# Expert tiles routed in two rounds: six tiles from the first three batches during attention, the rest beside those tiles

## The chip, the cores and the metric

The kernel runs on one core of a Trainium2 chip. A core has five engines, each with an instruction queue of its own that is worked in order: TensorE (PE in the profile; its weight loads are PEld), VectorE (DVE), ScalarE (ACT), GpSimd (POOL) and SyncE (SP), which here only issues transfers. Engines wait for one another through semaphores; the DMA engines move data beside all of them. TensorE reads its operands from the on-chip memory (SBUF) and writes its sums to PSUM, eight banks of 2 KB a partition. The metric is the time of one execution in microseconds on the device. `L12` in a line of the profile is line 12 of the kernel's file; the letters ahead of it name the engine.

## The reference

Sparse attention (half of the heads attend to the last 32 positions, half to every 32nd), and behind it a mixture of eight experts. A token takes the expert that its own logits prefer, or, where its local gate says so, the expert of the token before it. It then passes through that one expert and is scaled by that expert's probability.

```python
batch, n_heads, seq, head_dim = (8, 8, 576, 64)        # attention; float32 throughout
mask_local = (rel >= 0) & (rel < 32)                   # heads 0 to 3
mask_strided = (rel >= 0) & (pos[None, :] % 32 == pos[:, None] % 32)   # heads 4 to 7
attn = softmax(where(mask, q @ k.T / 8, -1e9))
x = (attn @ v).transpose(0, 2, 1, 3).reshape(8, 576, 512)

logits = x @ w_gate                                    # 8 experts
local_gate = sigmoid(x @ w_local)
for b in range(B):
    prev_e = -1
    for s in range(S):
        fresh_e = argmax(logits[b, s])
        e = fresh_e if s == 0 or local_gate[b, s] < 0.5 else prev_e
        prev_e = e
        p = softmax(logits[b, s])
        out[b, s] = p[e] * (relu(x[b, s] @ w1[e]) @ w2[e])   # w1[e] 512x1024, w2[e] 1024x512
```

## The kernel before

**Attention** (`attention`, L145) goes through 8 batches of 8 units (both counted from 0 below). A unit is a pair of heads and half of the sequence's blocks. Per unit, TensorE computes the scores (`L241`), ScalarE takes the exponential (`L245`), VectorE multiplies by the mask (`L248`), TensorE multiplies with the values (`L287`), and VectorE normalises into rows `xl` or `xs` (`L295`, `L297`, `L298`). The loop is written in a staggered order: step n issues the scores of unit n, the values of unit n-2, and, for every second unit, the transposes `turn_x` (`L321`, `L329`; ScalarE copies them to `xT`, `L323`, `L332`) of unit n-3. Each group of two pairs is stored to the DRAM table `xd` of 4608 rows of 512 numbers (`L306`, `L310`); a batch has six loads and six stores, all issued by SyncE. Behind a batch's last transposes stand its gates (`L334` to `L372`): eight matmuls with the gate weights (`L340`), a copy `gl` (`L343`), six small matmuls that turn the logits to token rows (`L346`), and VectorE's softmax and argmax. They leave `probs` (eight probabilities a token) and `codes`, a number from which the running maximum later tells each token's expert. Transposes, values and gates share one PSUM pool (`psT`, two tiles of two banks); scores have `psS`, also two tiles of two banks.

**Routing** (`route`, L397) runs once, after the last batch. It turns the codes to rows (`L442`, copied by `L446`), finds each token's expert by a running maximum (`L448`) and marks it one-hot (`L454`, `hot`), counts with a running sum (`cum`), rounds each expert's count up to whole tiles of 128 tokens, and gives each token a slot in the list of tiles. Then it inverts that list by 48 matmuls into a table (`L515`): `lane` marks a token's place within its tile, `put` its tile (`at`, `L505`) times its number and times its probability (`pt`, `L507`). The results are `gi` (which row of `xd` each slot gathers), `si` (which row of the output it writes, out of range for an empty slot), `ps_slot` (its probability) and `et` (the expert of each tile and the number of tiles used). After it a check (`bounds`) decides whether all sums were in a safe range; if not, everything would be done again more carefully, which does not happen here.

**Experts** (`experts`, L526) go tile by tile: two weight transfers of 2 MB (`L543`, `L545`, SyncE, from four buffers each), a gather of 128 rows (`L547`, GpSimd), four transposes (`L554`) and a copy (`L556`, VectorE), the hidden layer (`L566`, 64 matmuls counting the two passes that an fp32 one is recorded as; ScalarE's Relu `L568`), the output layer (`L574`), the scaling (`L577`) and a scatter to the output (`L578`, GpSimd). The loads of tile j+2 are issued ahead of tile j. At most 43 tiles can be needed and 36 always are; from tile 36 on each stands behind a branch on the count `used`:

```python
    for j in range(NT):
        if j == NT_MIN:
            used = nc.values_load(et[0:1, NT:NT + 1], min_val=NT_MIN, max_val=NT,
...
        if j + 2 < NT:
            load(j + 2)
        ...
            with tc.If(used > j):
                hidden(j)
                output(j)
```

The pools of routing and of the experts follow one another in the same part of SBUF and PSUM (the inner `ExitStack`s of `passes`, L105), so the first weight transfer waits until routing and the check are done with theirs. The order of each engine's queue is settled before the run by a scheduler from the program's order and its dependences.

## Time and profile before

| | us |
|---|---|
| median of three runs (866.14 to 867.58) | 867.15 |
| the profiled execution | 866.83 |
| its span | 865.10 |
| TensorE busy | 792.3 |
| VectorE busy | 170.2 |
| ScalarE busy | 154.1 |
| GpSimd busy | 90.1 |

The span is the time from the first to the last instruction that the profile shows; the execution's time lies 1.73 above it. Busy times are those of single engines and overlap. The rows that matter for the change, stage by stage and instruction by instruction, stand in the prediction. Four of its views need a word. The page's slices cut the span into 40 equal parts of 21.6 us, each a digit in tenths. A row of the windows gives `from:to`, the length, and each engine's busy time with its count, then TensorE's granted clock as a share of full speed, the share of 16 DMA engines busy, and GB/s. A row of the chain or of the timeline gives start and length of an instruction or of a run of like instructions, and in brackets the idle time before it and what ended it. A row of the groups ends with busy time, mean ns of one, and idle time before with its releaser.

### The profile page before, as it was taken

How to read it: one execution, taken by the hardware profiler on the slowest of the kernel's cores; microseconds unless marked ns; L12 is line 12 of the kernel's file. 1: busy time of each engine (PE TensorE's matmuls, PEld its weight loads, DVE VectorE, ACT ScalarE, POOL GpSimd, SP SyncE). 2: the span in 40 equal slices, each digit the busy share in tenths (PEclk: the TensorE clock that was granted, in tenths of full speed). 3: DMA queues.
4: the chain of work that ended last, by engine and by line, in shares of the span. 5: the costliest groups of instructions: out<-in, count | busy, mean ns of one | idle time of the engine just before them, and what ended most of it. 6: DMA issues, size and time to landing. Idle time of an engine off the chain costs nothing.

```text
span 865.1 us, 12699 instructions
## 1 busy us (share of the span) xinstructions
PE 792.3 (92%) x5324; PEld 605.3 (70%) x5324; DVE 170.2 (20%) x470; ACT 154.1 (18%) x250; POOL 90.1 (10%) x105
## 2 busy tenths in 40 slices
PE   6999999973859999999999999999999999997990
PEld 6777788762847777777777777777777777765860
DVE  4565665558320000000000000000000000000000
ACT  3444444430001111111111111111111111110110
POOL 1000000001030001111111111111111111110000
PEclk9999999985559999999999999999999999998995
DMA  9667776110079999999898989898989899886860
GB/s 363 237 236 236 236 236 233 58 56 1 0 276 399 399 400 399 400 399 375 320 339 312 340 313 336 318 339 315 331 311 341 307 338 322 330 318 216 299 227 8
DMA packets 91172, 242.63 MB, mean 280 GB/s; under 512 B 4638, under 2 KB 13854, under 8 KB 91104
## 3 DMA queue, kind: packets, MB, share of 16 engines
q1 hardware_dynamic: 83936, 220.92, 70.9%
q0 software_dynamic: 6640, 20.72, 6.3%
q8 instruction: 46, 0.75, 0.3%
q14 instruction: 22, 0.18, 0.1%
q10 hardware_dynamic: 528, 0.07, 0.0%
HBM read 222.81 MB, written 19.92 MB: 281 GB/s over the span
## 4 chain that ended last, share of the span: by engine, by line
issue 41%; PE 31%; DMA 15%; POOL 4%; ACT 3%; DVE 3%; POOLq 0%; SPq 0%; ACTq 0%
DMA out_dram<-y,si 13%; PE tps L287 9%; PE hps L566 5%; PE yps L574 5%; PE sps L241 4%; POOL out_dram L578 2%; PE tab L515 2%; POOL xg L547 2%; PE tps L340 2%; PE tps L329 1%; ACT xT L332 1%; ACT xT L323 1%; DMA xg<-xd,gi 1%; PE tps L346 1%; PE tps L321 1%
## 5 line engine op out<-in xcount | busy, mean ns | idle before, releaser
L566 PEld LDWEIGHTS hps<-xgT,w1t 128*128 128x128 f32 x2560 | 294.8, 193 | 17.8 <-issue 17.7
L566 PE MATMUL hps<-xgT,w1t 128*128 128x128 f32 x2560 | 295.0, 276 | 0.0
L574 PE MATMUL yps<-w2t,hT 128*128 128x512 f32 x640 | 281.3, 592 | 0.0
L574 PEld LDWEIGHTS yps<-w2t,hT 128*128 128x128 f32 x640 | 118.5, 190 | 133.9 <-issue 133.9
L556 DVE COPY xgT<-xps 128x512 f32<-128x512 f32 x43 | 29.6, 691 | 564.0 <-PE xps L554 503.0
L568 ACT ACTIVATE hT<-hps 128x512 f32<-128x512 f32 x80 | 47.8, 597 | 263.5 <-PE hps L566 263.5
L577 ACT ACTIVATE y<-yps,ps_slot 128x512 f32<-128x512 f32 x40 | 27.5, 687 | 264.9 <-PE yps L574 258.6
L578 POOL DMA_INDIRECT out_dram<-y,si x40 | 40.0, 1000 | 319.8 <-ACT y L577 305.5
L241 PE MATMUL sps<-qt,kt 64*128 64x96 f32 (+2 forms) x704 | 63.5, 295 | 6.6 <-DMA kt<-in_k_dram 6.6
L547 POOL DMA_INDIRECT xg<-xd,gi x43 | 42.3, 983 | 226.2 <-PE xps L554 200.9
L241 PEld LDWEIGHTS sps<-qt,kt 64*128 64x128 f32 (+2 forms) x704 | 47.8, 189 | 19.7 <-issue 11.2
L245 ACT ACTIVATE e<-sps 128x576 f32<-128x576 f32 (+1 forms) x64 | 41.8, 653 | 46.3 <-PE sps L241 35.5
L287 PE MATMUL tps<-vlt,e 128*96 128x96 f32 x384 | 40.9, 257 | 0.8
L554 PE MATMUL xps<-ident,xg 128*128 128x128 f32 x172 | 28.5, 295 | 13.8 <-DMA xg<-xd,gi 13.5
L287 PE MATMUL tps<-vst,e 108*108 108x108 f32 (+1 forms) x320 | 40.1, 273 | 0.7
L287 PEld LDWEIGHTS tps<-vlt,e 128*96 128x96 f32 x384 | 35.8, 167 | 4.0 <-ACT xT L323 2.3
L287 PEld LDWEIGHTS tps<-vst,e 108*108 108x108 f32 (+1 forms) x320 | 34.6, 180 | 4.4 <-ACT xT L323 2.2
L554 PEld LDWEIGHTS xps<-ident,xg 128*128 128x128 f32 x172 | 21.7, 152 | 16.9 <-issue 15.9
L248 DVE TENSOR_TENSOR e<-e,maskL 128x576 f32<-128x576 f32 x32 | 24.3, 758 | 36.3 <-ACT e L245 36.3
L515 PE MATMUL tab<-put,lane 96*128 96x86 f32 x96 | 20.8, 422 | 11.1 <-DVE put L507 11.1
L515 PEld LDWEIGHTS tab<-put,lane 96*128 96x128 f32 x96 | 20.6, 333 | 11.2 <-issue 11.2
L248 DVE TENSOR_TENSOR e<-e,maskS 108x648 f32<-108x648 f32 (+1 forms) x32 | 24.2, 757 | 16.8 <-ACT e L245 16.8
(133 smaller groups left out, 250.5 us busy)
## 6 DMA issues: line engine op xcount, KB each, us to landing
w1t<-in_w_dram SPq DMA_DIRECT2D x43, 2048.0 KB
w2t<-in_w_dram SPq DMA_DIRECT2D x43, 2048.0 KB
kt<-in_k_dram SPq DMA_DIRECT2D x16, 608.0 KB
qt<-in_q_dram SPq DMA_DIRECT2D x16, 576.0 KB
vlt<-in_vl_dram SPq DMA_DIRECT2D x8, 780.0 KB
vst<-in_vs_dram SPq DMA_DIRECT2D x8, 650.0 KB
xd<-xl SPq DMA_DIRECT2D x8, 576.0 KB
xd<-xs SPq DMA_DIRECT2D x24, 108.0 KB
```

What stands on the lines that cost most here:

```text
L241: nc.tensor.matmul(ps[0:kb, h, i * w:(i + 1) * w], lhsT=kt[r, u.i2, c:c + kb], rhs=qt[r, u.i2, c:c + w], start=True, stop=True)
L245: nc.scalar.activation(ev, ps[0:kb, :, 0:m * w], Act.Exp, bias=0.0, scale=1.0 / DH ** 0.5)
L248: nc.vector.tensor_tensor(blocks(ev, m), blocks(ev, m), mask, op=Alu.mult)
L287: nc.tensor.matmul(ps[0:w, h, o:o + w], lhsT=u.e[0:kb, h, i * w:(i + 1) * w], rhs=vt[0:kb, u.i2, u.t0 + i, c:c + w], start=True, stop=True)
L515: nc.tensor.matmul(tab, lhsT=lane[:, i], rhs=put[:, i], start=(i == 0), stop=(i == CM - 1))
L547: nc.gpsimd.indirect_dma_start(out=t["x"], out_offset=None, in_=xd, in_offset=bass.IndirectOffsetOnAxis(ap=gi[:, j:j + 1], axis=0))
L554: nc.tensor.transpose(ps[:, kk * P:(kk + 1) * P], t["x"][:, kk * P:(kk + 1) * P], ident)
L556: nc.vector.tensor_copy(t["xT"], ps)
L566: nc.tensor.matmul(ps[:, i], lhsT=t["w1"][:, kk, c], rhs=t["xT"][:, kk * P:(kk + 1) * P], start=(kk == 0), stop=(kk == DK - 1))
L568: nc.scalar.activation(t["hT"][:, g * HB:(g + 1) * HB], ps, Act.Relu)
L574: nc.tensor.matmul(ps, lhsT=t["hT"][:, kk], rhs=t["w2"][:, kk, :], start=(kk == 0), stop=(kk == FK - 1))
L578: nc.gpsimd.indirect_dma_start(out=out, out_offset=bass.IndirectOffsetOnAxis(ap=si[:, j:j + 1], axis=0), in_=y, in_offset=None, bounds_che ...
```

## The change

Routing is done twice by one generator, `route(..., nb, ...)`, which is resumed piece by piece from other code. The first time it takes the codes of three batches (`BE`) during the attention to the later ones, and yields six tiles (`NE`); experts are served in order, each with its whole tiles only, until six are taken (`tiles`), and `early` keeps how many tiles each expert has had. Tokens beyond those tiles get a slot that is out of range. The second time it takes all eight batches; tokens up to an expert's early tiles (`thr`) are out of range now, and the counts are lessened by them. `final` tells the two apart.

`passes` resumes the first routing every second unit from step 27 (behind the gates of the third batch), and from step 45 issues one of eight weight transfers of 1 MB (`pieces`, for tiles 0 and 1) and, for three tiles (`AHEAD`), a gather. `Experts.run` resumes the second routing three times in each of the tiles 0 to 2: twice between hidden layer and transposes, once behind the output layer.

```diff
+BE = 3
+NE = 6
+AHEAD = 3
...
+        ex = Experts(ctx, tc, xd, w1, w2, out, c, r1, r2)
         with ExitStack() as part:
-            experts(part, tc, xd, w1, w2, out, ident, gi, si, ps_slot, et)
+            psX = part.enter_context(tc.tile_pool(name="psX", bufs=2, space=PSUM))
+            rp = part.enter_context(tc.tile_pool(name="rp", bufs=1))
+            first = route(tc, rp, psX, BE, c, codes, r1, early)
+            pieces = ex.weights(0) + ex.weights(1)
+            for n in attention(part, tc, careful, psX, q, k, vl, vs, wg, xd, c, codes, sums):
+                n -= 8 * BE + 3
+                if n >= 0 and n % 2 == 0:
+                    next(first, None)
+                n -= 18
+                if n >= 0 and n % 2 == 0:
+                    if pieces:
+                        pieces.pop(0)()
+                    if n // 2 < AHEAD:
+                        ex.gather(n // 2)
+        with ExitStack() as part:
+            psr = part.enter_context(tc.tile_pool(name="psr", bufs=2, space=PSUM))
+            rp = part.enter_context(tc.tile_pool(name="rp2", bufs=1))
+            ex.run(part, route(tc, rp, psr, B, c, codes, r2, early),
+                   None if careful else lambda: bounds(tc, rp, psr, sums, bad))
```

The buffers of the experts are now held from the start, beside those of attention: two each of `w1t` and `w2t`, five of gathered rows, three of results.

```diff
+        self.w1t = Ring(xp, 2, [P, DK, F], "w1t")
+        self.w2t = Ring(xp, 2, [P, FK, D], "w2t")
+        self.xg = Ring(xp, AHEAD + 2, [P, DX], "xg")
+        self.xT = Ring(xp, 2, [P, D], "xgT")
...
+    def run(self, ctx, second, check):
...
+        self.psx = Ring(pp, 1, [P, D], "tps")
+        self.psh = Ring(pp, 3, [P, self.HB, P], "hps")
+        self.psy = Ring(pp, 2, [P, D], "yps")
+        used = None
+        self.turn_x(0)
+        for j in range(NT):
+            ahead = self.weights(j + 2) if j + 2 < NT else []
+            if j + AHEAD < NT:
+                self.gather(j + AHEAD)
+            if j == NE and check:
+                check()
+            if j >= NT_MIN:
+                if used is None:
...
+                ctx.enter_context(tc.If(used > j - NE))
+            self.hidden(j)
+            for piece in ahead[:2]:
+                piece()
+            if j < NE - AHEAD:
+                next(second, None)
+                next(second, None)
+            if j + 1 < NT:
+                self.turn_x(j + 1)
+            self.output(j)
+            for piece in ahead[2:]:
+                piece()
+            if j < NE - AHEAD:
+                next(second, None)
```

The branches from tile 36 on are now one inside the other, with the transfers of later tiles inside them.

The probability of a slot no longer comes through the table. A row of `xd` is 520 numbers wide; SyncE writes a batch's eight probabilities a token behind its 512 (one more transfer a batch, pieces of 32 bytes), the gather brings them along, and VectorE picks one by the tile's one-hot expert `oh`, in `turn_x` of the experts:

```diff
-        nc.vector.tensor_tensor(probs[:, :, b, :], ex, spread(sm, [LQ, LT, E]), op=Alu.mult)
+        nc.vector.tensor_tensor(ex, ex, spread(sm, [LQ, LT, E]), op=Alu.mult)
+        nc.sync.dma_start(out=xd[b * S:(b + 1) * S, D:DX].rearrange("(t p) e -> p t e", p=LQ), in_=ex)
...
+        nc.vector.tensor_copy(self.xT[j], ps)
+
+        nc.vector.tensor_tensor(self.pe[j], x[:, D:DX], t["rd"].oh[:, t["i"]], op=Alu.mult)
+        nc.vector.tensor_reduce(self.pt[j], self.pe[j], axis=AX.X, op=Alu.add)
```

In `route`, codes go to one row tile in two halves, both scans work with fewer passes around them, the fourfold `pt` and the one-hot transposes are gone, and `at`, `put` and `lane` are bf16, exact for these small whole numbers: `put` holds the token's column and its row separately, which are joined behind the table.

```diff
-    nc.vector.tensor_copy(run.rearrange("r (a x) -> r a x", a=2), cps[:, :, 0:S // 2])
+        nc.vector.tensor_copy(run[:, a * S // 2:(a + 1) * S // 2], ps[0:R, 0:S // 2])
+    nc.vector.tensor_tensor_scan(run, run, run, 0.0, Alu.max, Alu.max)
...
+    nc.vector.tensor_tensor_scan(cum, hot, hot, 0.0, Alu.add, Alu.max)
+    yield
...
+        nc.vector.tensor_scalar(tiles, first, -1.0, float(NE), Alu.mult, Alu.add)
+        nc.vector.tensor_tensor(tiles, tiles, nt, op=Alu.min)
+        nc.vector.tensor_copy(early, tiles[0:E])
...
+    at = rp.tile([LQ, CN, n], BF16, name="at")
...
+    put = rp.tile([LQ, CN, 2, n], BF16, name="put")
...
+    lanes((0, 1))
+    yield
+    lanes((2, 3, 4, 5))
+    yield
+    ps = bank()
+    tab = ps[:, 0:2 * n].rearrange("p (a n) -> p a n", a=2)
+    for i in range(CN):
+        nc.tensor.matmul(tab, lhsT=lane[:, i], rhs=put[:, i], start=(i == 0), stop=(i == CN - 1))
```

The constants of routing move to the program's start (`Consts`). To make room in PSUM and SBUF, the values of a unit go to one bank (`psV`, two of one bank; the two heads of a pair are swapped on the host and written so that they overlap), and the transposes, the gates and the first routing share `psX`, two of one bank, with a copy for each half; `rows` has one buffer in place of two, `small` three in place of four.

```diff
-    rows = ctx.enter_context(tc.tile_pool(name="rows", bufs=2))
-    small = ctx.enter_context(tc.tile_pool(name="small", bufs=4))
+    rows = ctx.enter_context(tc.tile_pool(name="rows", bufs=1))
+    small = ctx.enter_context(tc.tile_pool(name="small", bufs=3))
     psS = ctx.enter_context(tc.tile_pool(name="psS", bufs=2, space=PSUM))
-    psT = ctx.enter_context(tc.tile_pool(name="psT", bufs=2, space=PSUM))
+    psV = ctx.enter_context(tc.tile_pool(name="psV", bufs=2, space=PSUM))
```

The queues at three places. First TensorE from the last gates to the second tile. Before (`cps` to `tab` is the routing, `bps` the check):

```order
L340 MATMUL tps<-xT,wgs 32x288 x8
L346 MATMUL tps<-sel,gl 96x9 x6
L442 MATMUL cps<-ident,codes 64x96 x6
L461 MATMUL nps<-cum,same 64x1
L468 MATMUL nps<-nt,less 64x1
L491 MATMUL slps<-inb,slot 96x8 x6
L515 MATMUL tab<-put,lane 128x86 x48
L141 MATMUL bps<-one,low 1x1
L554 MATMUL xps<-ident,xg 128x128 x20
L566 MATMUL hps<-xgT,w1t 128x128 x32
L574 MATMUL yps<-w2t,hT 128x512 x8
```

The same place in the changed kernel (its own line numbers; `L412` and `L417` are the gates, `L663` an expert tile's transposes, `L677` its hidden and `L685` its output layer, `L486` to `L522` the second routing):

```order
L412 MATMUL xps<-xT,wgs 32x288 x8
L417 MATMUL xps<-sel,gl 96x9 x3
L663 MATMUL tps_2436<-ident,xg_137 128x128 x4
L417 MATMUL xps<-sel,gl 96x9 x3
L677 MATMUL hps_2437<-xgT_142,w1t_133 128x128 x16
L677 MATMUL hps_2438<-xgT_142,w1t_133 128x128 x16
L486 MATMUL xps<-ident,codes 64x96 x6
L663 MATMUL tps_2436<-ident,xg_138 128x128 x4
L685 MATMUL yps_2440<-w2t_135,hT_144 128x512 x5
L503 MATMUL xps<-cum,same 64x1
L504 MATMUL xps<-cum,before 64x1
L522 MATMUL xps<-nt,less 64x1
```

Tile 0 now stands directly behind the gates, its transposes among them, and the second routing's first matmuls stand behind tile 0's hidden layer; a further three matmuls of the output layer stand ahead of `L522`, and the second routing's 48 of the table behind tile 1.

Second, VectorE behind the first routing, at the border of batches 4 and 5 (`sums` and `rc` belong to the normalisation of a unit, `xl` and `xs` to its rows). Before:

```order
L295 TENSOR_SCALAR sums<-tps 126x2x2
L297 RECIPROCAL rc<-sums 126x2x2
L298 TENSOR_TENSOR xs<-tps,rc 126x2x2x64
L248 TENSOR_TENSOR e<-e,maskL 128x2x288
L295 TENSOR_SCALAR sums<-tps 108x6
```

The same place in the changed kernel (`pe` and `pt` pick the probability of a gathered row `xg`):

```order
L601 CAST gi<-rowf 128x6
L604 TENSOR_TENSOR si<-rowf,skip 128x6
L319 TENSOR_TENSOR e<-e,maskL 128x2x288
L367 TENSOR_SCALAR sums<-vps 108x6
L369 RECIPROCAL rc<-sums 108x6
L370 TENSOR_TENSOR xs<-vps,rc 108x2x3x64
L666 TENSOR_TENSOR pe_149<-xg_137,oh 128x8
L667 TENSOR_REDUCE pt_151<-pe_149 128x1
L319 TENSOR_TENSOR e<-e,maskL 128x2x288
L367 TENSOR_SCALAR sums<-vps 126x2x2
L666 TENSOR_TENSOR pe_150<-xg_138,oh 128x8
```

The picks for the first four gathered tiles stand in VectorE's queue from one unit behind the cast that gives the gathers their rows, between the masks and normalisations of attention.

Third, SyncE in the changed kernel, in batch 5 (`L288` to `L298` are loads of attention, `L378` and `L382` its stores, `L444` the probabilities, `L646` to `L649` the weights; an `ISA` row computes an address):

```order
L382 DMA xd<-xs 7x18x256 x2
L646 TENSOR_LOAD et
L649 ISA
L649 DMA w1t_133<-in_w_dram 128x2x1024
L288 DMA qt<-in_q_dram 128x1152
L444 DMA xd<-ex 96x6x8
L291 DMA kt<-in_k_dram 128x1216
L295 DMA vlt<-in_vl_dram 128x1560
L378 DMA xd<-xl 96x6x256
```

Before, only loads and stores of attention stand here; `et` is read, and weights are asked for, in their midst now.

470 lines of the change are left out of this document (245 added, 225 removed).

## The prediction

> **What bounds the kernel now.** I read the slices of the page first, then the busy time by stage, then the order in time at the stage borders.
>
> ```profile
> PE   6999999973859999999999999999999999997990
> PEclk9999999985559999999999999999999999998995
> DMA  9667776110079999999898989898989899886860
> ```
>
> TensorE is full except in slices 9 to 12 and at the end; in that hole its clock is at 0.5 and the DMA engines rest for two slices. So the kernel is TensorE-bound with one hole between attention and experts. The stages:
>
> ```profile
> core 0: us, PE busy (x) PEld busy (x) DVE busy (x) ACT busy (x) POOL busy (x), PEclk, DMA share, GB/s
> 36.03:171.50 135.47, 131.05 (x1359) 108.56 (x1358) 82.77 (x270) 57.78 (x96) 0.00 (x0) 1.00 0.62 206
> 171.50:191.70 20.20, 17.68 (x158) 13.66 (x157) 10.14 (x38) 7.36 (x12) 0.00 (x0) 0.92 0.20 60
> 191.70:243.10 51.40, 28.72 (x144) 27.61 (x144) 30.08 (x73) 0.44 (x2) 7.12 (x7) 0.52 0.01 2
> 243.10:254.94 11.84, 5.26 (x21) 3.78 (x21) 2.21 (x4) 0.00 (x0) 4.89 (x6) 0.50 0.93 343
> 341.57:356.02 14.45, 14.45 (x86) 10.62 (x86) 0.69 (x1) 1.88 (x3) 1.99 (x2) 1.00 1.04 400
> 774.91:784.67 9.76, 2.57 (x18) 2.06 (x16) 1.29 (x2) 0.69 (x1) 3.90 (x4) 0.78 0.89 297
> 784.67:842.97 58.30, 58.30 (x329) 42.60 (x328) 2.77 (x4) 6.84 (x11) 3.02 (x3) 0.98 0.69 238
> 842.97:865.10 22.13, 0.00 (x1) 0.00 (x0) 0.00 (x0) 0.69 (x1) 0.98 (x1) 0.55 0.03 8
> ```
>
> Attention (row 1) is six batches of 22.58 us, TensorE 97% busy: 4.4 us idle in six, 0.73 a batch. VectorE is 61% busy, 13.8 us a batch, so 8.8 us a batch are free. Rows 3 and 4 are the hole, 63.24 us. A tile (row 5) is 14.45 us of unbroken TensorE. The borders, in order of time:
>
> ```profile
> 190.51 1.19 PE L346 MATMUL tps<-sel,gl 128*96 128x9 f32 x12 [0.73 <-ACT gl L343]
> 219.05 20.75 PE L515 MATMUL tab<-put,lane 96*128 96x86 f32 x96 [11.12 <-DVE put L507]
> 243.17 0.44 SPq L543 DMA_DIRECT2D w1t<-in_w_dram  x1
> 254.94 7.26 PE L566 MATMUL hps<-xgT,w1t 128*128 128x128 f32 x50
> 835.94 7.03 PE L574 MATMUL yps<-w2t,hT 128*128 128x512 f32 x16
> ```
>
> The gates end at 191.70, the first weight transfer is issued at 243.17, after routing and the check of the sums, the first expert matmul runs at 254.94, the last ends at 842.97. So 588.03 us are tiles and 22.13 end the program. The profiled execution took 866.83 us, 1.73 over its span; the median shown is 867.15, 0.3 higher.
>
> **The change, term by term.** I move the start of the first tile, then the tiles, then the end.
>
> *The hole.* After the change, TensorE's row behind the last gates is tile 0, whose weights and rows were asked for during attention.
>
> ```profile
> 255.15 8.62 PE hps L566 x64
> 263.76 6.87 PE yps L574 x16
> 270.63 7.14 PE hps L566 x64
> 341.41 7.31 PE L566 MATMUL hps<-xgT,w1t 128*128 128x128 f32 x64
> 355.86 7.31 PE L566 MATMUL hps<-xgT,w1t 128*128 128x128 f32 x64
> L556 DVE COPY xgT<-xps 128x512 f32<-128x512 f32 x43 | 29.6, 691 | 564.0 <-PE xps L554 503.0
> ```
>
> The last two rows of TensorE give a tile's 14.45 (355.86 - 341.41); the rows above split it into 7.14 hidden, 6.87 output, and so 0.44 for four transposes. Between the last gates and tile 0 stand these transposes and the copy `L556`, 0.69 and a release, of which three of the gate matmuls cover about half: 0.44 + 0.45 = 0.9 in place of 63.24. What hides the routing that stood there is told in the next terms; what hides the 11.84 us of loading is attention, and the price if that cover fails is those 11.84.
>
> *First routing, inside attention.* TensorE there is full, so its work counts in full; VectorE's is hidden in the 8.8 free us a batch, if it comes in time.
>
> ```profile
> 102.57 1.19 PE L346 MATMUL tps<-sel,gl 128*96 128x9 f32 x12 [0.17 <-ACT gl L343]
> 94.56 0.43 PE L329 MATMUL tps<-ident,xs 126*128 126x126 f32 x2 [0.19 <-ACT xT L332]
> L446 DVE COPY run<-cps 64x576 f32<-64x576 f32 x1 | 0.7, 740 | 0.0
> L448 DVE TENSOR_TENSOR_SCAN last<-run 64x576 f32<-64x576 f32 x1 | 1.4, 1350 | 0.0
> L454 DVE TENSOR_SCALAR hot<-hot,er 64x576 f32<-64x576 f32 x1 | 0.5, 510 | 0.0
> L505 DVE TENSOR_TENSOR at<-io,hi 96x2064 f32<-96x2064 f32 x1 | 2.3, 2298 | 0.0
> L507 DVE TENSOR_TENSOR put<-at,pt 96x2064 f32<-96x2064 f32 x1 | 5.8, 5755 | 0.0
> L512 DVE TENSOR_TENSOR lane<-io,lo 96x1024 f32<-96x1024 f32 x6 | 7.1, 1213 | 0.0
> ```
>
> A small fp32 pass is 0.1 us (12 for six matmuls in 1.19). The first round has 16 fp32 matmuls, 32 passes, 3.2 us, and 18 bf16 ones. No row shows a bf16 matmul: 0 below, above the table pass of now at full clock (20.75 / 96 x 0.5 = 0.108). I take 0.08: 1.5 us. Sum 4.7. VectorE gets about 15 us: the chain to `cum` is two copies, two scans and three passes (0.7 + 2.7 + 1.5 = 4.9), lanes of 384 columns 6 x 0.5, the rest some 35 instructions of 0.15 to 0.8. It comes in 14 units (39.5 us, of which VectorE has 15.4 free): nearly full. TensorE meets `L503` about 5 us of its own work after `L486`, while VectorE needs 4.9 plus its masks: a stall of 1 to 2.
>
> *First gathers.* Their `pe` product stands in VectorE's queue one unit behind `gi`, ahead of the masks and normalisations of the next units.
>
> ```profile
> L547 POOL DMA_INDIRECT xg<-xd,gi x43: 944/987/1167, 240.8 to 779.6; - x43
> DMA to landing us min/median/max: 3.4/7.1/8.3
> ```
>
> A gather takes 3.4 to 8.3 us to land and four leave about 1.3 apart, so the fourth lands 7.3 to 12.2 after `gi`, where VectorE would be in some 5: it stands 2.5 to 7. A unit's values come two units after its scores (5.6 us), so about 3.5 is absorbed: 0 to 3.5 reach TensorE, 1.5 taken. Stalls in all: 3.0, from 0 to 15 (all of VectorE's work). Against it, transposes get banks of their own: the waits of row `L329` are part of the 0.73 idle a batch, of which I take half, 2.9 in eight batches (0 to 5.8), and 1.0 of the drain after 182 (0 to 2).
>
> *Transfers and other queues.* SyncE issues eight weight pieces of 1 MB among the last three batches' loads and stores: 8.4 MB in some 75 us are 112 GB/s on top of the 206 of the attention row, 318 where the tile row reaches 400. Each load leads its use by a batch, 22.6 us, so I cost this at nothing; were that cover gone, a late load would cost its own few microseconds, up to 5. The eight-column probabilities are a thirteenth transfer beside a batch's twelve, behind the stores, and nobody waits for them but gathers long after. GpSimd's queue holds only gathers in attention. The constants of routing, moved to the very start, lie beside the first load:
>
> ```profile
> PE sps L241 <- DMA kt<-in_k_dram: 6.6, 1, 6.6
> ```
>
> Tile 0 so starts at 191.70 + 0.9 + 4.7 + 3.0 - 2.9 - 1.0 = 196.4, **58.5 earlier**.
>
> *Tiles.* Still 40: the inputs give the experts 234, 210, 229, 189, 269, 118, 264 and 215 tokens in the first three batches, nine whole tiles, so six are full, and the rest round up as before.
>
> ```profile
> 783.79 1.09 PE L554 MATMUL xps<-ident,xg 128*128 128x128 f32 x4 [6.84 <-DMA xg<-xd,gi]
> ```
>
> 40 x 14.45 = 578.0. A cold first tile cost 8.62 - 7.14 = 1.5; I add 1.0 (0 to 1.7). Second routing: 18 fp32 matmuls, 36 passes, 3.6, and 48 bf16 ones, 4.0 (0 to 5.2): 7.6. Its waits: the chain to `cum` is the 4.9 of the first round, the copy for tile 1 in its midst (0.69) and half a microsecond of releases, 6.1 after `L486`; TensorE has four transposes and ten passes of tile 0's output to do, 0.44 + 10 x 6.87 / 16 = 4.7: it stands 1.5. The tables have 14.45 us until TensorE wants them and need some 14 (`at` 2.0, two `put` 3.5, lanes 7.3, small ones 1.5): 0.5; at the 5.8 of `L507` for both `put` it would be 8. The wait of 6.84 at tile 36 goes, since its gather is issued three tiles ahead; the load of `used` stays: 1.0 (0 to the 7.2 that TensorE idles in that row's stage). Sum 589.6 against 588.03: **+1.6**.
>
> *End.* Weights of tile 41 are asked for when tile 39 frees its buffer, and SyncE's closing branch waits for them.
>
> ```profile
> 844.02 0.98 POOL L578 DMA_INDIRECT out_dram<-y,si  x1 [13.95 <-ACTq L598]
> SPq L645 <- DMA out_dram<-y,si: 19.4, 1, 19.4
> ```
>
> 2 MB at 400 GB/s are 5.2 us beside the last output transfer: **+2.0** (from -3, with two branches fewer, to +7).
>
> 866.83 - 58.5 + 1.6 + 2.0 = 811.9, so **812**. The ends of the unknown terms, one at a time: stalls in attention 809 to 824, PSUM waits 809 to 815, late loads to 817, the bf16 passes 806 to 814, the tables' wait to 819, `used` 811 to 818, the end 807 to 817.
>
> *A rule weighed.* TensorE's clock in the drain:
>
> ```profile
> 182.00:186.00 4.00, 2.74 (x25) 2.30 (x23) 2.05 (x8) 1.74 (x3) 0.00 (x0) 1.00 0.08 20
> 187.00:189.00 2.00, 2.00 (x15) 0.83 (x16) 0.00 (x0) 0.59 (x1) 0.00 (x0) 0.50 0.38 114
> 190.00:191.70 1.70, 1.19 (x12) 1.09 (x12) 0.00 (x0) 0.45 (x1) 0.00 (x0) 1.00 0.04 14
> ```
>
> It fell to 0.5 after four microseconds at 69% busy and was back by 190. The Trainium skill ("TensorE: Matmul & The Clock Gate", What's actually happening) has the clock halve only after an idle window of about 3.4 us; the drain has none, so by the rule tile 0 starts at full clock and the sum is 811; the row says that a partly idle stretch is enough, hence my 1.0.
>
> **The rivals.** *VectorE holds attention up* (chance 0.20). For it: 15.1 us into 15.4 free, gathers of up to 8.3 in an in-order queue. Against: the two units of slack. If half of the 15 and the whole 7 of the gathers reach TensorE it is 14.5 in place of 3.0: **824**, from 818 to 836.
>
> On this the Trainium skill ("SBUF — State Buffer", SBUF: two separate sides) adds that VectorE's two-port operations lock GpSimd out of writing gather descriptors. The rows show 1167 ns against a median of 987 for the gather issued beside VectorE's casts, 0.2 us each; it moves 0.02 of chance to this rival.
>
> *Everything hides* (0.12): no stalls, all 0.73 a batch gained, no waits in the second routing, shorter end: 811.9 - 3.0 - 3.9 - 2.0 - 4 = **799**.
>
> *The first round is not six full tiles* (0.03): each empty one costs 14.45; one gives **826**. The counts above speak against it.
>
> *Slower: two weight buffers* (0.02). Today four are in turn; then w1 of tile j+2 is asked for when j's first matmuls end and wanted 6.87 + 0.44 + 14.45 = 21.8 us later. The stage row shows 400 GB/s, 5.2 us for 2 MB. To eat 55 us in 38 tiles each would have to lose 1.45, a load of 24.7 us: 85 GB/s. Beyond that point it would be slower, at **875**.
>
> **How the numbers follow.** Forecast 0.62 (804 to 820), VectorE 0.20, everything hidden 0.12, an empty tile 0.03, slower 0.02, and 0.01 for the weight rival stopping just at its break-even, which would read as the same. The range, 801 to 828, takes in every single end above and most of the two near rivals; it leaves out about 0.16: three quarters of the lower rival, a fifth of the upper and what lies at no gain. What this kernel's measurement can tell from no change is about 0.2%, 1.7 us. The first four cases are all faster: 0.97; same 0.01, slower 0.02.
>
> **What would show it.** No slice with TensorE under 8 between attention and tile 0; tile 0 at 193 to 200 us; a batch still 22.2 to 22.6 us outside the routed ones, and 4 to 10 us more in those together; VectorE waiting for `xg` in batches 4 and 5; tiles of 14.45 from tile 3 on, none waiting for `w1t`; 7 to 10 us more in the first three; SyncE's last wait on `w1t` or `w2t`. It would be wrong if a batch grows by over 5 us, or if tiles lie over 14.6 apart.

## The result and the profile after

The changed kernel took **798.94 us** (median of four runs, 796.14 to 801.12) against 867.37 for the kernel before (four runs by then): a ratio of 0.921 (95% interval 0.9175 to 0.9249), 68.4 us less. The prediction of 812 (801 to 828) had the sign, and the mechanism for the hole, but the time lies 2 us under its range. The profiled execution took 797.11, its span 795.30. Its slices:

```profile
PE   6999998999999999999999999999999999999990
PEclk9999999999999999999999999999999999999995
DMA  9687688883789899998998998989989989889892
```

The hole in slices 9 to 12 is gone, and so is the half clock in it. The windows below go from gates to gates of a batch (the first four: batches 2 to 5) and from tile to tile (the last four: tiles 0 to 3):

```profile
core 0: us, PE busy (x) PEld busy (x) DVE busy (x) ACT busy (x) POOL busy (x), PEclk, DMA share, GB/s
...
53.08:74.37 21.29, 21.10 (x226) 17.96 (x226) 13.57 (x46) 9.74 (x20) 0.00 (x0) 1.00 0.79 244
74.37:100.14 25.77, 24.82 (x259) 20.98 (x259) 20.37 (x75) 9.84 (x20) 0.00 (x0) 1.00 0.66 217
100.14:124.89 24.75, 22.17 (x244) 18.78 (x244) 15.81 (x61) 10.36 (x20) 4.92 (x5) 0.97 0.86 278
124.89:146.63 21.74, 21.56 (x228) 18.15 (x226) 15.11 (x50) 9.37 (x20) 0.00 (x0) 0.96 0.85 287
...
189.26:206.90 17.64, 16.89 (x105) 12.19 (x105) 9.81 (x32) 1.53 (x4) 0.44 (x1) 1.00 0.61 203
206.90:223.16 16.26, 16.26 (x102) 12.22 (x101) 9.91 (x22) 1.78 (x3) 1.02 (x1) 1.00 0.70 241
223.16:239.33 16.17, 16.17 (x133) 12.33 (x132) 7.32 (x14) 1.88 (x3) 8.19 (x4) 1.00 0.82 283
239.33:253.78 14.45, 14.45 (x85) 10.63 (x84) 1.02 (x3) 1.88 (x3) 1.99 (x2) 1.00 0.95 335
```

A batch without routing takes 21.29 where it took 22.57. Batches 3, 4 and 5, which carry the first routing and the gathers, take 72.26 together, 8.4 more than three others. Tiles 0 to 2, which carry the second, take 6.72 more than three of 14.45. The borders on TensorE, from the timeline (start, length, and in brackets the idle time before):

```profile
188.31 0.60 PE L417 MATMUL xps<-sel,gl 128*96 128x9 f32 x6
189.26 7.41 PE L677 MATMUL hps<-xgT,w1t 128*128 128x128 f32 x64 [0.35 <-DVE xgT L664]
...
203.43 0.24 PE L503 MATMUL xps<-cum,same 64*64 64x1 f32 x2 [0.74 <-DVE cum L497]
...
230.31 1.85 PE L595 MATMUL xps<-put,lane 96*128 96x74 bf16 x48
...
767.43 7.03 PE L685 MATMUL yps<-w2t,hT 128*128 128x512 f32 x16
```

The last gate ends at 188.91 and tile 0 follows after 0.35. The last matmul ends at 767.43 + 7.03 = 774.46; the 20.84 us from there to the end of the span (795.30) end the program. Against the prediction, term by term:

| term | predicted | measured |
|---|---|---|
| between the last gates and tile 0 | 0.9 | 0.35 |
| first routing with its stalls | +7.7 | +8.4 |
| PSUM waits of attention (measured: all that a batch got shorter) | -2.9 | -9.9 |
| drain and its clock | -1.0 | -1.3 |
| start of tile 0 | 196.4 | 189.26 |
| tiles (588.03 before) | +1.6 | -2.8 |
| end (22.13 before) | +2.0 | -1.3 |
| the profiled execution | 811.9 | 797.1 |

The 9.9 are 0.81 in the first batch, 7.74 in the six that follow (1.29 each) and 1.36 in the last up to its gates. The 1.3 of the drain are the last gates themselves: 4.80 us from their first matmul to the end before, in good part at half clock, and 3.51 now.

### The profile page after: what moved, and what is told of

Its sections match the earlier page's. It is cut to its first block, busy times and chain, and to the rows that moved or that the text cites. A ratio compares the mean times of both kernels' runs of the same rounds, so it can differ in the third digit from the quotient of the medians.

```text
span 795.3 us, 13159 instructions
## 1 busy us (share of the span) xinstructions
PE 761.4 (96%) x5308; PEld 580.6 (73%) x5308; DVE 186.7 (23%) x599; ACT 155.2 (20%) x273; POOL 89.9 (11%) x104
## 4 chain that ended last, share of the span: by engine, by line
PE 90%; DMA 3%; issue 2%; DVE 2%; ACT 1%; POOL 0%; SPq 0%; POOLq 0%
PE hps L677 34%; PE yps L685 32%; PE vps L359 9%; PE sps L312 6%; PE tps L663 2%; DMA out_dram<-y,si 2%; PE xps L396 2%; PE xps L412 2%; PE xps L417 1%; DMA xg<-xd,gi 1%; ACT xT L402 1%; DMA kt<-in_k_dram 1%; DVE cum L497 0%; DVE run L490 0%; PE xps L486 0%
## 5 line engine op out<-in xcount | busy, mean ns | idle before, releaser
L677 PEld LDWEIGHTS hps<-xgT,w1t 128*128 128x128 f32 x2560 | 291.9, 192 | 18.2 <-issue 17.7
L677 PE MATMUL hps<-xgT,w1t 128*128 128x128 f32 x2560 | 292.6, 275 | 0.3 <-DVE xgT L664 0.3
L685 PE MATMUL yps<-w2t,hT 128*128 128x512 f32 x640 | 281.6, 593 | 0.0
L685 PEld LDWEIGHTS yps<-w2t,hT 128*128 128x128 f32 x640 | 118.5, 190 | 133.4 <-issue 133.3
L664 DVE COPY xgT<-tps 128x512 f32<-128x512 f32 x41 | 28.4, 692 | 246.1 <-PE tps L663 246.0
L687 ACT ACTIVATE y<-yps,pt 128x512 f32<-128x512 f32 x40 | 27.5, 687 | 272.3 <-PE yps L685 272.3
L667 DVE TENSOR_REDUCE pt<-pe 128x1 f32<-128x8 f32 x41 | 6.5, 159 | 247.9 <-ACT y L687 247.8
L359 PE MATMUL vps<-vlt,e 128*96 128x96 f32 x384 | 41.5, 258 | 0.0
L359 PE MATMUL vps<-vst,e 108*108 108x108 f32 (+1 forms) x320 | 40.3, 273 | 0.0
L359 PEld LDWEIGHTS vps<-vlt,e 128*96 128x96 f32 x384 | 36.0, 168 | 3.5 <-issue 0.3
L359 PEld LDWEIGHTS vps<-vst,e 108*108 108x108 f32 (+1 forms) x320 | 34.7, 180 | 3.0
L663 PE MATMUL tps<-ident,xg 128*128 128x128 f32 x164 | 24.8, 274 | 0.0
L402 ACT COPY xT<-xps 128x324 f32<-128x324 f32 (+1 forms) x32 | 18.8, 676 | 17.3 <-PE xps L396 17.3
L663 PEld LDWEIGHTS tps<-ident,xg 128*128 128x128 f32 x164 | 19.2, 142 | 0.1
```

The source lines that it names most:

```text
L359: nc.tensor.matmul(ps[0:w, o:o + w], lhsT=u.e[0:kb, h, i * w:(i + 1) * w], rhs=vt[0:kb, u.i2, u.t0 + i, c:c + w], start=True, stop=True)
L663: nc.tensor.transpose(ps[:, kk * P:(kk + 1) * P], x[:, kk * P:(kk + 1) * P], self.c.ident)
L664: nc.vector.tensor_copy(self.xT[j], ps)
L677: nc.tensor.matmul(ps[:, i], lhsT=w1[:, kk, c], rhs=xT[:, kk * P:(kk + 1) * P], start=(kk == 0), stop=(kk == DK - 1))
L685: nc.tensor.matmul(ps, lhsT=self.hT[j][:, kk], rhs=self.w2t[j][:, kk, :], start=(kk == 0), stop=(kk == FK - 1))
L687: nc.scalar.activation(y, ps, Act.Copy, scale=self.pt[j])
```

## The experiments

Three questions stood open. Was it the layout of PSUM that shortened every batch, by more than the idle time shown there? What are the 8.4 us of the first routing, and why do the changed kernel's executions fall into two groups, 796 to 797 and 801, with granted clocks of 0.99 and 0.98? And which of the terms for the tiles and the end were off, and why?

**The changed kernel again.** No edit.

> The changed kernel once more, unaltered. Its four executions lay at 796.1, 797.1, 800.8 and 801.1 us with granted clocks of 0.989, 0.987, 0.980 and 0.980. If the gap of 4 us comes from where the gathers land in attention (theory: VectorE waits for them, TensorE then stands and its clock falls), both groups come again, and a profile of a longer one shows more than the 2.57 us stall in batch 4, followed by a lower clock. If it is noise of the whole chip, the times spread evenly and the kernel before spreads as much.

Measured: 795.16, 795.42, 795.78, 799.32 and 799.76, while eleven runs of the kernel before on that chip spread from 864.3 to 869.0 without a gap. The profile is of a longer one (799.32). TensorE's stall in its batch 4, from the timeline:

```profile
122.63 0.41 PE L396 MATMUL xps<-ident,xs 126*128 126x126 f32 x2 [3.01 <-DVE pe L666]
```

Its windows of two microseconds at that place:

```profile
122.00:124.00 2.00, 1.37 (x13) 0.99 (x17) 0.61 (x4) 1.50 (x3) 0.00 (x0) 0.85 0.49 186
124.00:126.00 2.00, 2.00 (x18) 0.76 (x10) 1.44 (x5) 0.52 (x2) 0.00 (x0) 0.50 0.70 167
...
130.00:132.00 2.00, 2.00 (x14) 1.83 (x15) 1.26 (x6) 0.54 (x2) 0.00 (x0) 0.50 0.28 107
132.00:134.00 2.00, 2.00 (x19) 1.81 (x20) 0.99 (x7) 0.66 (x1) 0.00 (x0) 0.59 0.15 11
```

The same windows in the shorter execution, the one profiled with the result:

```profile
122.00:124.00 2.00, 0.36 (x2) 0.29 (x2) 1.49 (x7) 0.00 (x0) 0.00 (x0) 0.85 0.91 287
124.00:126.00 2.00, 2.00 (x18) 1.16 (x20) 0.44 (x3) 0.58 (x1) 0.00 (x0) 0.50 0.52 188
126.00:128.00 2.00, 2.00 (x24) 1.14 (x16) 1.37 (x4) 0.80 (x2) 0.00 (x0) 0.80 0.97 269
```

The column behind GpSimd's is the clock. Summed over windows of half a microsecond, its time at 0.5 is 3.42 us in the shorter execution, behind a stall of 2.57, and 10.24 us in the longer one, behind a stall of 3.01. At half clock 3.42 us lose 1.7 us of work and 10.24 lose 5.1; the difference of 3.4 is most of the 4.3 between the means of the two groups (795.9 and 800.2 over the nine executions). The length of the stall does not set that of the stretch: in three later profiles with the gathers in a row, stalls of 2.42 (`no_tail_loads`), 2.91 (`tables_fp32`) and 3.38 us (`ahead2`) were followed by 10.24, 10.24 and 13.66 us. All these stretches are one, three or four times 3.41, and so is the first one in the drain of the kernel before (3.41, from 186).

The Trainium skill ("TensorE: Matmul & The Clock Gate", What's actually happening) has the clock set by a free-running window of about 3.4 us, so that what follows a stall varies from run to run. The two groups and the whole multiples agree with that. Ten microseconds at half clock with TensorE busy throughout, where by the same section some 3.4 of sustained work bring it back, do not, and neither do stalls of 2.42 to 3.01 us that bring it down, where by that section it takes an idle window of that length.

**Picks behind the transposes.** In the trace of the changed kernel, VectorE waits for the first gather and TensorE then for VectorE:

```profile
121.72 0.17 DVE L666 TENSOR_TENSOR pe<-xg,oh 128x8 f32<-128x8 f32 x1 [4.31 <-DMA xg<-xd,gi]
...
123.64 0.65 PE L396 MATMUL xps<-ident,xs 126*128 126x126 f32 x2 [2.57 <-DVE xs L370]
```

In the program the picks stand behind attention (`turn_x`); it is the scheduler that put them into batch 4. So they were given a value to wait for, made from their tile's transposes.

```diff
         nc.vector.tensor_copy(self.xT[j], ps)
-        nc.vector.tensor_tensor(self.pe[j], x[:, D:DX], t["rd"].oh[:, t["i"]], op=Alu.mult)
+        nc.vector.tensor_scalar(self.one[j], self.xT[j][:, 0:1], 0.0, 1.0, Alu.mult, Alu.add)
+        nc.vector.scalar_tensor_tensor(self.pe[j], x[:, D:DX], self.one[j], t["rd"].oh[:, t["i"]], Alu.mult, Alu.mult)
```

> The picks of the slots' probabilities (pe, pt) are tied behind the copy of their tile's transposes, one small VectorE instruction more per tile. Theory (in attention, VectorE's queue is held by the picks, which wait 4.31 us for the first gather, and TensorE stands 2.57): the stall goes, batches 4 and 5 fall from 24.75 and 21.74 to about 22.0 and 21.5, and the time falls by 2.5 to 3.5 us against the changed kernel, with less spread. Rival (VectorE's own load of routing holds attention up, the gathers only show it): batch 4 stays within 0.5 us and the time within 1 us.

Measured: 793.76, 794.75 and 795.76, and 799.47, 800.25 and 800.51: both groups still there. The timeline of the place:

```profile
121.25 0.41 PE L396 MATMUL xps<-ident,xs 126*128 126x126 f32 x2 [0.81 <-issue]
...
122.48 0.65 ACT L316 ACTIVATE e<-sps 128x576 f32<-128x576 f32 x1 [4.11 <-PE xps L396]
...
123.80 1.59 PE L412 MATMUL xps<-xT,wgs 128*32 128x288 f32 x16 [1.75 <-ACT xT L402]
```

VectorE's wait is gone, but TensorE still stands 0.81 + 1.75 = 2.56 us. Now it is ScalarE that begins an exponential after 4.1 us of idle time, 3.5 us after its scores were done at 118.97. The engine that the profile named was not the only one held, and removing its wait gained nothing that can be told. What was left in common was five gathers, issued one behind the other from 114.95 to 121.23. ScalarE's late start is not in every such profile: it stands in this one and in the longer execution of the changed kernel, while in the other four with the gathers in a row the exponential starts on time and VectorE's wait alone goes with TensorE's stall.

**Gathers spread out.** The picks as in the run before, and each of the first five gathers waits for the normalisation of a unit.

```diff
+AFTER = {0: 43, 1: 45, 2: 47, 3: 52, 4: 57}
...
+        if j in AFTER:
+            n = AFTER[j]
+            self.nc.vector.scalar_tensor_tensor(self.tied[:, j:j + 1], self.sums[:, n, 0, 0:1], 0.0, index,
+                                                Alu.mult, Alu.add)
+            index = self.tied[:, j:j + 1]
```

> As late_pick, and the first five gathers are no longer issued one behind the other in batch 4, but each behind the normalisation of a unit (43, 45, 47, 52, 57), by a small VectorE instruction that makes its indices. In late_pick the picks were gone, yet TensorE still stood 0.81 + 1.75 us in batch 4, behind a ScalarE that stood 4.1 us with its scores ready, while GpSimd issued five gathers in 6.3 us. Theory (five gathers in a row are what holds the engines there, whichever queue shows it): no stall over 1 us in batches 4 to 6, the clock stays at 1.00 there, batches 4 and 5 at about 22.0 and 21.5, and the time is 2 to 3 us under the shorter times of late_pick (793.8 to 795.8), 791 to 793, without a second group 4 us above. Rival (the stall belongs to the place, to what SyncE or the instruction supply do there): the stall stays at the same place and both groups of times come again.

Measured: 792.42, 793.72, 793.97 and 794.61, median 793.84, a ratio of 0.9151 to the kernel before (0.9138 to 0.9164): one group, the clock at 0.989 or 0.990 in all four. Batches 3 to 5:

```profile
74.43:100.19 25.76, 24.81 (x259) 20.99 (x259) 20.36 (x75) 9.82 (x20) 0.00 (x0) 1.00 0.68 217
100.19:121.92 21.73, 21.54 (x245) 18.50 (x245) 16.81 (x60) 9.86 (x20) 0.00 (x0) 1.00 0.79 262
121.92:143.21 21.29, 21.10 (x226) 17.97 (x227) 13.68 (x49) 9.74 (x20) 3.02 (x3) 1.00 0.90 298
```

Batch 4 takes 3.0 us less than in the changed kernel, batch 5 0.45 less, and no stall stands there, so the theory holds. The edit also moves the gathers: they are issued from 132 to 172 us, not from 115 to 121. Five in a row at a later place were not run, so that it is their spacing and not their place remains an argument. This is the fastest version made here: 3.3 us under the median of the changed kernel's nine executions (797.11), and about 2 under the shorter of them.

**Gathers spread out, picks early.** The fourth case of two by two: as the last, with the changed kernel's own line for `pe` restored.

> As spread_gathers, but the picks of the probabilities are again where the changed kernel has them: in VectorE's queue one unit behind each gather's indices. The fourth case of two by two: gathers in a row or spread, picks early or late. Theory (five gathers in a row are the trouble; a gather by itself lands in some 3.5 us and a pick one unit behind it holds VectorE for 1 to 2 us, which the two units of slack take up): no stall of TensorE over 1 us, clock 1.00, time within 1.5 us of spread_gathers' 793.8. Rival (the picks are trouble by themselves): VectorE waits 3 us or more for each of four gathers, TensorE stands in batches 5 to 7, 3 to 8 us more.

Measured: 804.86 (799.61 to 807.75). The waits of VectorE in batches 4 to 7, and two of the places where TensorE stands behind them:

```profile
DVE pe L675 <- DMA xg<-xd,tied: 14.2, 4, 6.0
```

```profile
139.63 0.41 PE L397 MATMUL xps<-ident,xs 126*128 126x126 f32 x2 [2.64 <-DVE xs L371]
...
167.93 1.23 PE L360 MATMUL vps<-vlt,e 128*96 128x96 f32 x12 [3.48 <-issue]
```

The rival holds in the main: early picks are trouble by themselves. They wait 14.2 us for four gathers, up to 6.0 for one, and as the gathers are apart now, so are the stalls. The profile is of the shortest execution, and the loss by the median, 11 us, is more than the rival's 3 to 8. The row at 167.93 names no releaser, but VectorE's wait of 6.0 ends at 166.10, and its normalisation behind that (`xs`), the last to read the bank that these values take, ends at 167.83. In a row, the first pick's wait of 4.31 covered most of the others' (0.78 and 1.28 behind it). So both had to go: taking the picks alone showed no gain that can be told, taking the row alone a loss.

**The first routing thinner.** As with spread gathers, but resumed every third unit, the gathers two to six units later (behind units 49, 51, 53, 56 and 59).

```diff
-                if n >= 0 and n % 2 == 0:
+                if n >= 0 and n % 3 == 0:
                     next(first, None)
```

> As spread_gathers, but the first routing is resumed every third unit in place of every second, and the five gathers follow two batches later (behind units 49, 51, 53, 56 and 59). Batch 3 takes 25.77 us against 21.28 for one without routing; its routing passes on TensorE are 2.75, so 1.74 are waits. Theory (they come from VectorE, 20.4 of 25.8 us busy in that batch): with the same work over more units the batches 3 to 5 together take 1 to 2 us less, 792 to 793. Rival (they are releases between engines, as many however the steps lie): the sum of the batches stays within 0.5 us, as does the time.

Measured: 794.93 (794.51 to 795.55), 1.1 us more. Batches 3 to 5, and three shorter windows in batch 4:

```profile
73.33:97.67 24.34, 23.48 (x244) 19.64 (x244) 18.45 (x65) 9.95 (x20) 0.00 (x0) 1.00 0.66 209
97.67:122.52 24.85, 24.65 (x241) 21.05 (x241) 18.34 (x64) 9.89 (x20) 0.00 (x0) 0.93 0.76 246
122.52:144.24 21.72, 21.53 (x245) 18.47 (x245) 14.06 (x52) 9.74 (x20) 0.00 (x0) 1.00 0.85 284
```

```profile
106.00:108.00 2.00, 2.00 (x19) 1.65 (x19) 1.21 (x7) 0.00 (x0) 0.00 (x0) 0.87 0.47 79
108.00:110.00 2.00, 2.00 (x13) 1.97 (x12) 0.86 (x2) 0.59 (x1) 0.00 (x0) 0.50 0.72 272
110.00:112.00 2.00, 2.00 (x22) 1.76 (x21) 1.75 (x7) 0.58 (x1) 0.00 (x0) 0.77 0.58 238
```

The three take 70.91 against 68.78, so neither theory holds. The clock fell to 0.5 for 3.42 us with TensorE shown as busy, at the end of the twelve three-column passes of `L562` (`L559` in the changed kernel), which run from 106.3 to 107.4; that is 1.7 us of the 2.1. Those short passes alone do not make it fall: the same twelve leave it at 1.00 in the eight other profiles of the changed kernel and its variants. What did stays open. That VectorE's load makes batch 3's waits is not borne out.

**The PSUM layout alone**, in the kernel before. Values go to `psV` and transposes and gates to `psX`, as in the change (with the heads swapped on the host); routing and experts are as before.

```diff
-    psT = ctx.enter_context(tc.tile_pool(name="psT", bufs=2, space=PSUM))
+    psV = ctx.enter_context(tc.tile_pool(name="psV", bufs=2, space=PSUM))
+    psX = ctx.enter_context(tc.tile_pool(name="psX", bufs=2, space=PSUM))
```

> The kernel before, with only the PSUM part of the change: values in one bank with two buffers of their own, transposes and gates in two others with a copy for each half. Theory (the layout alone takes 1.28 us off each batch, since values no longer wait for a bank that ScalarE's copy still reads; waits that the idle time of a batch, 0.73, shows only in part): batches of 21.3, about 10 us less than the kernel before, 857. Rival (the prediction's: no more than the shown idle can go, half of it likely): 2.9 to 5.8 us less, 861.5 to 864.5.

**Only the values apart**: `psV` as above, but for transposes and gates one pair of banks with one copy over both, and the code of before.

```diff
-    psT = ctx.enter_context(tc.tile_pool(name="psT", bufs=2, space=PSUM))
+    psV = ctx.enter_context(tc.tile_pool(name="psV", bufs=2, space=PSUM))
+    psT = ctx.enter_context(tc.tile_pool(name="psT", bufs=1, space=PSUM))
```

> The kernel before, with the values in one bank with two buffers of their own, but transposes and gates still with one copy each over two banks, of which there is one pair. Theory (it is the values that waited for ScalarE's copies): batches of about 21.8, 5 to 8 us less than the kernel before. Rival (what counts is that a copy is made of each half, so that transposes and gates go on): 0 to 3 us less, or more time than before, since transposes and gates now have one pair of banks in place of two.

Measured: 856.26 (855.60 to 857.02) with the layout and 857.03 (855.64 to 857.85) with the values apart, against 866.85 before: ratios of 0.9882 (0.9862 to 0.9903) and 0.9883 (0.9861 to 0.9904), 10.6 and 9.8 us less. Two successive gates in the one, then in the other:

```profile
53.43 1.60 PE L342 MATMUL xps<-xT,wgs 128*32 128x288 f32 x16 [0.19 <-ACT xT L332]
74.72 1.60 PE L342 MATMUL xps<-xT,wgs 128*32 128x288 f32 x16 [0.19 <-ACT xT L332]
```

```profile
54.44 1.18 PE L342 MATMUL tps<-xT,wgs 128*32 128x288 f32 x16
75.50 1.18 PE L342 MATMUL tps<-xT,wgs 128*32 128x288 f32 x16
```

Batches of 21.29 and of 21.06, where the kernel before has 22.57. So the layout by itself is worth the 10 us, and the values in banks of their own are enough for it. Halves with a copy each add nothing that the time shows: they cost 0.23 a batch and give back 1.2 in the drain, whose last gate matmul ends at 180.45 with them and at 181.69 without. The wait of the values can be seen in the kernel before, where they begin as ScalarE's copy of the transposes ends (62.36 + 0.64 = 63.00):

```profile
61.20 0.48 PE L241 MATMUL sps<-qt,kt 64*126 64x126 f32 x2
61.61 0.71 PE L321 MATMUL tps<-ident,xl 96*128 96x96 f32 x6
62.25 0.70 PE L241 MATMUL sps<-qt,kt 64*126 64x126 f32 x8
62.36 0.64 ACT L323 COPY xT<-tps 128x576 f32<-128x576 f32 x1 [1.46 <-PE tps L321]
...
63.05 1.26 PE L287 MATMUL tps<-vlt,e 128*96 128x96 f32 x12
64.24 0.81 PE L241 MATMUL sps<-qt,kt 64*108 64x108 f32 x10
...
71.99 0.43 PE L329 MATMUL tps<-ident,xs 126*128 126x126 f32 x2 [0.19 <-ACT xT L332]
```

In the changed kernel the values follow the same eight passes 0.64 after their start, not 0.80:

```profile
60.52 0.71 PE L312 MATMUL sps<-qt,kt 64*126 64x126 f32 x8
61.16 1.26 PE L359 MATMUL vps<-vlt,e 128*96 128x96 f32 x12
```

No bracket stands at 63.05, and idle time is only 0.10 of those 0.16: the ends of pipelined passes are modelled, and the last of them covers part of the wait. In the batch as a whole TensorE's idle time fell by 0.54 and its *busy* time by 0.74, for the same passes. But this wait comes only twice a batch. Laid side by side from start to start, like passes of a batch take (us):

| stretch of a batch | before | changed | values apart |
|---|---|---|---|
| second values behind the gates to the fourth (60.01 to 64.98 before) | 4.97 | 4.27 | 4.26 |
| from there to the sixth (64.98 to 69.51) | 4.53 | 4.36 | 4.37 |
| first transposes `L329` to the next values (70.74 to 72.75) | 2.01 | 1.43 | 2.01 |
| second transposes `L329` to the second values behind the gates (53.18 to 60.01) | 6.83 | 6.99 | 6.19 |
| the rest | 4.24 | 4.24 | 4.23 |

The values' wait for the copy is 0.16 in each of the first two rows, 0.32 of 1.29 a batch. The third row is the wait that the prediction had named, the transposes' for ScalarE's copy of the half before: in the changed kernel it goes with the halves, worth 0.58 where 0.19 was shown idle; with only the values apart it stays, and as much is gained elsewhere. The rest lies where the scheduler, given other buffers, found another order. Before, it cut the scores of two units into pieces of two passes (61.20), eight and ten, which take 0.41, 0.80 and 0.74 to the next start, where eight and twelve take 0.64 and 0.76; with the values apart, ten value passes stand between the gates and their small matmuls. How much is waiting and how much is order these runs cannot part: the old order with the new banks was not run. The passes of the values, whose order and place in the bank the edit changes too, take as long as before, 1.26 for twelve.

**The tables in fp32**, in the second routing alone.

```diff
+    tt = F32 if final else BF16
...
-    at = rp.tile([LQ, CN, n], BF16, name="at")
+    at = rp.tile([LQ, CN, n], tt, name="at")
```

(and likewise `put` and `lane`)

> The second routing's at, put and lane in fp32, as the kernel before has them; the first routing's stay bf16. Theory (the 48 bf16 passes of the table took 1.7 us, 0.035 each; 96 fp32 passes at full clock are 0.108 each by the kernel before, 10.4 us, and VectorE's put, 2.0 + 0.67 us in bf16, grows towards the 5.8 of before, which makes TensorE wait a few us more): 9 to 13 us more than the changed kernel. Rival (the prediction's price of 0.08 for a bf16 pass, so that fp32 adds 6.4, and no wait): 6 to 7 us more.

Measured: 811.14 (808.59 to 811.42). The profile is of the shortest, with the clock at 0.983; its span of 806.9 is 9.3 over that of the changed kernel's second profile (797.6 at 0.984). TensorE's table in this run:

```profile
233.03 10.84 PE L596 MATMUL xps<-put,lane 96*128 96x74 f32 x96
```

From its start to the next row it takes 10.68 us, against 232.00 - 230.31 = 1.69 in bf16: +9.0, and no wait stands ahead of it. So a bf16 matmul is 0.035 us, not 0.08, and the rival with the prediction's price falls; of the theory the price held, and the waits that it added did not come. By the Trainium skill ("TensorE: Matmul & The Clock Gate", Wait — 56ns, not 53.3ns?) one of 74 columns takes an estimated 74 / 2.4 GHz and 2.5 ns, 0.033 us, and the trace agrees.

**Gathers two tiles ahead**, with the second routing still in tiles 0 to 2.

```diff
-AHEAD = 3
+AHEAD = 2
...
-            if j < NE - AHEAD:
+            if j < 3:
```

> Gathers are issued two tiles ahead, as before, in place of three (and two of them in attention); the second routing stays in tiles 0 to 2. Theory (the wait of 6.84 us at tile 36 went because the gather is now issued three tiles ahead): the wait comes back, the time is 5 to 7 us longer than the changed kernel's. Rival (it went because the transposes of the next tile now stand inside the branch, so that TensorE no longer runs ahead to gathers that were only just issued): no idle time at tile 36, time within 1 us of the changed kernel's.

Measured: 795.45, 800.32, 801.02 and 803.27, the two groups of the changed kernel. The profile is of the longest; its batch 4 stands 3.38 us. Tile 36:

```profile
721.41 7.31 PE L677 MATMUL hps<-xgT,w1t 128*128 128x128 f32 x64
728.55 0.60 PE L663 MATMUL tps<-ident,xg 128*128 128x128 f32 x4
```

No idle time. TensorE's queue tells why. Before, the transposes of four tiles stood ahead of the first branch, so that TensorE ran on to gathers only just issued (the last at 779.65; the transposes that waited 6.84 us begin at 783.79):

```
L574 MATMUL yps<-w2t,hT 128x512 x8
L554 MATMUL xps<-ident,xg 128x128 x16
L586 TENSOR_LOAD et
L598 COMPARE_AND_BRANCH
L566 MATMUL hps<-xgT,w1t 128x128 x32
```

In the changed kernel each tile's transposes stand inside the branch of the tile ahead of it. The rival holds: the lead of the gathers isn't what took the wait away. That the nesting did is what the two queues say; it was not tried alone.

**No loads for tiles 40 to 42.** Those tiles are not used with this input; their weights are left out.

```diff
-            ahead = self.weights(j + 2) if j + 2 < NT else []
+            ahead = self.weights(j + 2) if j + 2 < 40 else []
```

> The weights of tiles 40 to 42 are not loaded (with this input 40 tiles are used, 0 to 39, so the output is the same). Theory (the last 4 MB, issued up to 771 us, land beside the last scatter and its landing, and cost nothing): the end from the last matmul stays at 20.8 us, time within 1 us of the changed kernel's. Rival (the prediction's: SyncE's closing branch waits for them): the end is 2 to 5 us shorter.

Measured: 794.25, 797.55, 798.69 and 798.75. From the last scaling (ScalarE's `y`) to the end of the span, in this run 795.8 - 777.71 = 18.1:

```profile
777.71 0.69 ACT L687 ACTIVATE y<-yps,pt 128x512 f32<-128x512 f32 x1 [6.65 <-PE yps L685]
```

In the changed kernel it is 795.3 - 774.50 = 20.8, and 20.8 in its second profile. The loads cost 2.7 us there, within what the rival gave. By the run times it is less, 1.7 in the shorter group (794.25 against a mean of 795.9) and 1.9 in the longer (798.3 against 800.2).

## Why the prediction was off

**The hole and what replaces it: right.** 63.24 us became 0.35 (0.9 forecast), behind an attention that carries routing, gathers and weights. No transfer was late: nothing in the trace shows TensorE waiting for `w1t` or `w2t`, and tiles from 3 on are 14.45 apart, but for two that take 0.1 and 0.2 more. Two weight buffers were enough, so the slower rival had nothing behind it.

**The step that failed is the term for the PSUM waits.** The prediction put them inside the idle time of a batch ("the waits of row `L329` are part of the 0.73 idle a batch, of which I take half, 2.9 in eight batches (0 to 5.8)"), and so had a batch stay at 22.2 to 22.6 us. It became 21.29: the term was 9.9, and by itself, in the kernel before, 10.6, more than the bound. Idle time was no bound, since busy time fell too, by 0.74 a batch. Of the 1.29 a batch, the first of the two waits of the row that it named gave 0.58, three times the idle time shown there; the values' waits, which have no bracket in the trace, gave 0.32; the rest lies where TensorE's queue came out in another order, which the prediction did not ask about. How the gain parts between waits and order stays open. The 7.0 us by which the term was too small are nearly half of the 14.8 by which the sum missed.

**First routing: the total right, the shares not.** 8.4 against 7.7. Its matmuls are about 3.2 by the timeline (4.7 forecast); the stalls, with the clock that they cost, 5.2 (3.0). The mechanism of the gathers was as described, VectorE waiting ahead of masks and normalisations: 4.31 us, of which 2.57 reached TensorE (1.5 forecast, 0 to 3.5). Not foreseen was that taking the picks away doesn't end the stall, and that the clock behind it stands at half for one, three or four stretches of 3.41 us, of which each loses 1.7.

**Tiles: three terms too dear.** The table's bf16 price (1.7 in place of 4.0), the waits of the second routing (0.74 in place of 2.0), and 1.0 each for a cold start and for `used`, of which half a microsecond is left over in all. The clock is 1.00 from the last gates on, so the rule of the Trainium skill that was weighed in the prediction gave the better number for tile 0 than its row of the drain. It was no test of the rule: TensorE is busier in the drain now (3.26 of the 4 us from 182 to 186, against 2.74), and stalls of 2.42 to 3.01 us in batch 4, shorter than the rule's idle window, did bring the clock down. That the wait at tile 36 goes was right, its reason ("since its gather is issued three tiles ahead") wrong: with two tiles it goes as well.

**End: +2.0 forecast, -1.3 measured.** The loads do cost 2.7, but the end without them, from the last scaling on, is 3.9 shorter than the kernel before's (18.1 against 22.0); the prediction had that gain as an end of its range, not in its sum. What in the end became shorter wasn't tried.

Of the rivals, "everything hides" came within a microsecond of the time, 799, yet not for its reasons: it had stalls at nothing and the PSUM waits at 5.8, so that its nearness is luck. The forecast's range took the end of each unknown term one at a time; here the PSUM waits, the tiles and the end all missed to the same side, by 7.0, 4.4 and 3.3.

## What to carry to other kernels

Idle time in a trace of pipelined matmuls is no bound on what waits cost: compare start to start with an undisturbed run of like passes, and trace PSUM banks to the engine that reads them last. New buffers also give a scheduler a new order, so look at the queue before putting a gain down to a wait. Work that waits for a transfer does not belong in the in-order queue of an engine that feeds the critical one, and a scheduler may put it there though the code has it far behind; give it something late to wait for. Where a stall has two causes at one place, removing one shows nothing, so test them two by two.

## What was not expected of the hardware

The half clock came in whole stretches of 3.41 us. Behind stalls of TensorE of 2.4 to 3.5 us it lasted 3.42 us (twice), 10.24 (three times) and 13.66 (once), though TensorE was shown busy behind the stall; a stall of 2.64 in `spread_early`, and one of 2.56 in two pieces in `late_pick`, left it at 1.00. In `spread_thin` it came, 3.42 us long, with no idle time shown ahead of it. So these stalls do not say by their length whether the clock falls or for how long.

With five gathers of 128 rows issued in 6.3 us, ScalarE began an exponential 3.5 us after its scores were done (`late_pick`), and 4.1 us of like idle time stand before it in the second profile of the changed kernel; with the gathers apart there is no such wait. What ScalarE waited for the profile doesn't show, and it stays open. A late load of instructions does not end it: in `late_pick` the trace has transfers of instructions at 114.8 and 128.2 us, and none between.
